# First four weight tiles turned by quarters beside the gradient's quarters; bias loads and row-table inverse later

## The chip, the cores and the metric

One core of a Trainium2 chip runs the whole program. The metric is device time in microseconds of one execution; lower is better. Three executions of the kernel before took 340.55 to 341.36 us, median 341.02.

A core has five engines that run side by side, each in the order of its own instruction list: TensorE (PE; its weight loads are shown as PEld), VectorE (DVE), ScalarE (ACT), GpSimd (POOL) and SyncE (SP), which issues most DMAs. An instruction that waits holds up everything behind it on its engine.

## The reference

The program computes a network block, forward and backward, for one sample x of S = 2048 rows and D = 448 columns, with a hidden width F = 1792. Cut to what matters:

```python
h  = x + irfft2(rfft2(layernorm(x)) * (w_r + 1j * w_i))        # spectral filter
u  = gelu(einsum("bsd,sf->bdf", layernorm(h), w1) + b1)        # mixes the rows (tokens)
y  = einsum("bdf,fs->bds", u, w2) + b2
out = h + transpose(y)
# outputs: out, and the gradients of x, w_r, w_i, w1, b1, w2, b2 for a given grad_out
```

The backward pass needs dgu = w2 applied to grad_out, that is, for every block j of 128 hidden units, the sum over all 16 row tiles t of w2[j, t] times grad_out[t]. This product needs nothing but inputs, so the kernel uses it as filler work for TensorE while the Fourier transforms are going.

## The kernel before

The Fourier transform along the 2048 rows is split in two, with tables of cosines and sines that the kernel computes itself (Sin on ScalarE). The program goes through these stages: the **row stage** (both first transforms, per tile t of rows, to about 49 us), the second transform and the filter (`s2_stage`), the inverse rows (`inv_rows`), the layer norm of h, the two products with w1 and w2, and then the backward pass through the same steps.

For TensorE, SyncE, VectorE and ScalarE the order of the instructions is the order in which the Python code writes them (`manual_schedule`, L155); a planner places GpSimd's only. What happens around the change:

- `xn` holds x, `go_tp` holds grad_out by row tiles; both are loaded in quarters of 4 tiles by SP at the start (`load_x` L325, `load_go` L328). x's first quarter comes as two halves (L331, L333).
- `w2Ts[j]` is block j of w2 with its rows and columns exchanged tile by tile ("turned"), 16 tiles of 128x128. `load_w2T` (L303) loads blocks 0 to 4 as they are (`N_NAT`, into rB), and TensorE turns them with `turn_w2` (L314): eight transposes into a PSUM buffer, then one ScalarE copy to rE or rO. From block 5 on, a transposing DMA loads them turned. A ring of five places holds the blocks, so block j + 5 is loaded once block j has been used. From the ninth on (`CAP`) these loads are held back until the row stage is over (L960 to L962).
- `dg_gen` (L828) issues the fillers: one 128x128 by 128x448 matmul for each (j, t). In it, `turns` (L830) says after which filler a block is turned, `order` (L831) goes over blocks 0 and 1 by quarters of t, and the rest block by block. `fill(n)` (L792) issues the next n fillers. `evac` (L184) moves a finished sum out of PSUM with ScalarE or VectorE, whichever has the smaller planned load.
- The row stage (L871 to L952) has for each row tile t: statistics (`ln_stats`, VectorE), a table scaled by the row's norm (`scale_R`, VectorE), a fold (`fold_prep` or `fold_quarters`, VectorE), `row_a` (L660: four matmuls, one evac), and three steps later `row_b` (L670: four matmuls, one evac, one reshuffling DMA by SP). `FILL_A` and `FILL_B` (L908, L909) say how many fillers go between.
- The tables of the column transform, `csF`, are made in two parts: `gen_fwd_d` (L438) computes angles on VectorE, and `cs_ops`, run at t = 1 (L933 to L936), puts a Sin on ScalarE, two mirrored copies on VectorE, and last a copy of one column on ScalarE (L454).
- `gen_RT` (L523) makes the inverse of the row table: four ScalarE copies (L904 to L907), one matmul, one evac; it runs at t = 2 (L949).
- `load_biases` (L813) loads b1 and b2 as rows; they are turned into columns later (`turn_biases`, L1026).
- 20 matmuls on zeros (L374) keep TensorE busy until the first data is there.
- PSUM has two sets of four buffers: `ps_ff` and `ps_mm`. A new tile waits until the tile that had its buffer is emptied.

Of the kernel before, what the change touches and what calls it, by code (L numbers as in the profile page):

```python
# [10 lines left out]
BF16 = mybir.dt.bfloat16  # L11
# [6 lines left out]
P = 128  # L18
S = 2048
D = 448  # L20
# [15 lines left out]
ML_F = 4  # L36
SIDE = 2
CAP = 9
N_NAT = 5
U_Q = 2  # L40
N_FILL_F = (6, 3, 20, 3, 24, 2)
N_FILL_B = (16, 16, 26, 8, 24, 8)
# [82 lines left out]
def kernel(  # L125
# [47 lines left out]
    def ring(reg, off, count, *dims):  # L173
        n = int(np.prod(dims))
        return Ring([cut(reg, off + i * n, *dims) for i in range(count)])
# [122 lines left out]

    x_pt = A_x[0].rearrange("(p t) d -> p t d", t=NT)
    go_pt_d = grad_out[0].rearrange("(p t) d -> p t d", t=NT)  # L300
    w2T_ring = Ring(ring(rE, 0, 3, NT, P).views + ring(rO, S, 2, NT, P).views)

    def load_w2T():  # L303
        j = w2T_ring.i
        if j == NFB:
            return
        wT = w2T_ring.next()
        w2Ts[j] = wT
        if j < N_NAT:
            nc.sync.dma_start(out=w2n[j], in_=B_w2[j * P:(j + 1) * P, :].rearrange("f (t c) -> f t c", c=P))  # L310
            return
        nc.sync.dma_start_transpose(out=wT, in_=B_w2[j * P:(j + 1) * P, :].rearrange("f (t c) -> f t c", c=P))

    def turn_w2(j, parts=((0, 8), (8, 8))):  # L314
        for h, n in parts:
            pt = (ps_mm if j < 2 else ps_ff)()[:].bitcast(BF16).rearrange("p (t c) -> p t c", c=P)
            for t in range(n):
                nc.tensor.transpose(pt[:, t, :], w2n[j][:, h + t, :], ident[:])
            sc.copy(out=w2Ts[j][:, h:h + n, :], in_=pt[:, 0:n, :])

    go_tp_d = grad_out[0].rearrange("(t p) d -> p t d", p=P)
    w2Ts = {}
    w2n = [cut(rB, j % 4 * S, NT, P) for j in range(N_NAT)]

    def load_x(q):  # L325
        nc.sync.dma_start(out=xn[:, 4 * q:4 * q + 4, :], in_=x_pt[:, 4 * q:4 * q + 4, :])
# [2 lines left out]
        nc.sync.dma_start(out=go_tp[:, 4 * q:4 * q + 4, :], in_=go_tp_d[:, 4 * q:4 * q + 4, :])  # L329

    nc.sync.dma_start(out=xn[:, 0:2, :], in_=x_pt[:, 0:2, :])  # L331
    load_w2T()
    nc.sync.dma_start(out=xn[:, 2:4, :], in_=x_pt[:, 2:4, :])  # L333
    load_go(0)
    load_w2T()
    load_x(1)
    load_go(1)
    load_go(2)
    load_go(3)
    load_w2T()  # L340
    load_x(2)
    load_w2T()
    load_x(3)
    gtail = rst[0:16, 2 * P:3 * P]
    gp_.memset(gtail, 0.0)
    nc.sync.dma_start(out=gtail[:, 0:64], in_=grad_out[0][S - 16:S, 3 * P:D])


    s1, s128, s2048 = 2.0 * _sin_scale(2), _sin_scale(128), _sin_scale(2048)
# [21 lines left out]
    sc.activation(out=warm, in_=warm, func=ACT.Sin)  # L371
    nc.vector.memset(rAT[:, 0:512], 0.0)
    idle = ps_mm()
    for _ in range(20):  # L374
        nc.tensor.matmul(idle[:, 0:D], lhsT=rAT[:, 0:P], rhs=rAT[:, 0:D], start=True, stop=True)

    pcol = col()
# [434 lines left out]

    def load_biases():  # L813
        gp_.memset(smr, 0.0)
        nc.sync.dma_start(out=smr[0:NFB, 0, :], in_=B_b1.rearrange("(j p) -> j p", p=P))
        nc.sync.dma_start(out=smr[:, 1, :], in_=B_b2.rearrange("(j p) -> j p", p=P))

        def turn():
            for i, dst in ((0, b1col), (1, b2col)):
                nc.sync.dma_start_transpose(out=smc[:, i, :], in_=smr[:, i, :])  # L820

        def place():
            for i, dst in ((0, b1col), (1, b2col)):
                ve.tensor_copy(out=dst[:], in_=smc[:, i, :])
        return turn, place


    def dg_gen():  # L828
        pgs = {}
        turns = {(0, 3): 1, (1, 11): 2, (2, 4): 3, (3, 4): 4}  # L830
        order = [(j, 4 * q + i) for q in range(4) for j in range(2) for i in range(4)]  # L831
        for j, t in order + [(j, t) for j in range(2, NFB) for t in range(NT)]:
            if not t:
                pgs[j] = ps_mm()
            mm(pgs[j][:, 0:D], lhsT=w2Ts[j][:, t, :], rhs=go_tp[:, t, :], start=(t == 0), stop=(t == NT - 1))
            if (j, t) in turns:
                turn_w2(turns[j, t], ((0, 4), (4, 4), (8, 8)) if j == 0 and t == 3 else ((0, 8), (8, 8)))
            if t == NT - 1:
                evac(out=dgu[:, j, :], in_=pgs.pop(j)[:, 0:D])
                if w2T_ring.i >= cap[0]:  # L840
                    held_w2.append(load_w2T)
                else:
                    load_w2T()
            yield
# [29 lines left out]
    fold_prep(xn, 0)  # L874
    ve.reciprocal(out=rstd_x[:, 0:2], in_=rstd_x[:, 0:2])
    Rs = {t: scale_R(t) for t in range(2)}
    turn_w2(0, ((0, 4), (4, 4)))
    row_a(0, Rs.pop(0))
    for t in range(2, 4):
        ln_stats(xn, t, mvx)  # L880
    sc.activation(out=rstd_x[:, 2:4], in_=mvx[:, 2:4, 1], func=ACT.Sqrt, bias=eps_x, scale=1.0)
    turn_w2(0, ((8, 8),))
    fold_prep(xn, 1)
    cs_ops = []
    gen_fwd_d(cs_ops)
# [3 lines left out]
    uv = gen_UV()  # L889
    gen_inv_cols(0)  # L890
    gen_inv_cols(1)
    fill(4)
    for t in (4, 5):
        ln_stats(xn, t, mvx)
    for fn in rstd_of(4, 6):
        fn()
    fill(0)
    turn_biases, place_biases = load_biases()
    Meter.side, Meter.every, Meter.count = [], 1, 0
    GROUPS = {0: (6, 8), 1: (8, 10), 3: (10, 12), 5: (12, 14), 7: (14, 16)}  # L900
    STATS = {0: (6, 7), 1: (8, 9), **{t: (t + 8,) for t in range(2, 8)}}
    INV_S = {10: 0, 11: 1, 12: 2, 13: 3}
    W_AT = {0: 2, 1: 1, 2: 2, 3: 1, 4: 2, **{t: 1 for t in range(5, 11)}, 11: 4}
    for c in range(2):  # L904
        for e in range(2):
            sc.copy(out=Rp.rearrange("p (e a q b c) -> p c e a q b", e=2, c=2, q=8, a=2)[:, c, e],
                    in_=Rm[:, 64 * c + 32 * e:64 * c + 32 * e + 32].rearrange("p (q a b) -> p a q b", q=8, a=2))  # L907
    FILL_A = (4, 4, 8, 12, 6, 3, 3, 3, 3, 3, 3, 3, 3, 3, 3, 3)  # L908
    FILL_B = (0, 0, 2, 2, 2, 2, 4, 4, 3, 2, 2, 2, 2, 2, 2, 2)  # L909
    for t in range(NT):  # L910
        if t == 0:
            load_w2T()
        if t + 1 < NT:
            row_a(t + 1, Rs.pop(t + 1))
        fill(FILL_A[t])
        if 1 <= t and t + 3 < NT:
            if t + 3 in (4, 8, 12):
                while Meter.side:
                    Meter.side.pop(0)()
            Rs[t + 3] = scale_R(t + 3)  # L920
        row_b(t - 3, csQ if t - 3 >= 4 * U_Q else None)
        if t == NT - 1:
            for i in range(t - 2, NT):
                row_b(i, csQ)
        if t % 2 and t < 12:
            if t // 2 + 2 < 2 * U_Q:
                fold_prep(xn, t // 2 + 2)
            else:
                fold_quarters(xn, t // 2 + 2, t // 2 % 2 * 2)
        if t == 4:  # L930
            for w in range(2):
                gp_.tensor_copy(out=csQ[:, w, :, :], in_=csF[:, w, 0, :].rearrange("p (j e) -> p e j", e=2))
        if t == 1:  # L933
            sc.activation(out=warm, in_=half_r, func=ACT.Sin, scale=1.0 / 64.0)
            while cs_ops:
                cs_ops.pop(0)()  # L936
        for i in STATS.get(t, ()):
            ln_stats(xn, i, mvx)
        for _ in range(3 if t > 0 else 0):
            if next(uv, None):  # L940
                break
        if t in GROUPS:
            a, b = GROUPS[t]
            newton_gp(mvx[:, a:b, 1], rstd_x[:, a:b], slice(a, b))
        for _ in range(W_AT.get(t, 0)):
            next(w_loads, None)
        if t in INV_S:
            gen_inv_s(INV_S[t])
        if t == 2:  # L949
            gen_RT()  # L950
        fill(FILL_B[t])
    for _ in uv:  # L952
# [7 lines left out]
    cap[0] = NFB  # L960
    while held_w2:
        held_w2.pop(0)()  # L962
    fill(14)

    def fwd_mult(s, j, x, y):
# [486 lines left out]
```

## Time and profile before

| | |
|---|---|
| median of 3 executions | 341.02 us (340.55 to 341.36) |
| the profiled execution: its time | 340.96 us |
| its span (first to last instruction) | 339.2 us |
| TensorE busy | 330.3 us (97%) |
| VectorE, ScalarE, GpSimd busy | 252.6, 206.2, 83.9 us |
| granted TensorE clock | 0.999 of full speed |
| moved by DMA | 78.03 MB |
| TensorE busy in 0:10, 10:20, 20:30, 30:40, 40:50 us | 8.09, 9.06, 9.80, 9.07, 10.00 us |

The page gives the busy time of each engine, a chain of work followed back from the last instruction, and groups of instructions; the trace behind it answers for any stretch of time what each engine did, what it waited for, and which instruction or transfer ended the wait. All times are microseconds from the start of the span. A matmul's length includes its way through the array, so successive matmuls overlap; what counts for the order of things is the distance from one start to the next.

### The profile page before, as it was taken

To read this page: it belongs to the slowest core of one execution; us is meant where nothing else is said; L and a number is where in the kernel's file an instruction comes from. 1 tells how busy PE (TensorE), PEld (TensorE's weight loads), DVE (VectorE), ACT (ScalarE), POOL (GpSimd) and SP (SyncE) were. 2 spreads that over 40 slices of the span, in tenths; PEclk is the share of its full clock that TensorE was granted. 3 is DMA by queue.
4 is the path that set the end of the run, shared out by engine and by line. 5 is a ranking of instruction groups with operands and counts; after the bars stand their busy time and mean duration, and the time that the engine had idled before them with its cause. 6 is when DMAs were issued, how large, how long until landed. Compare 5 with 4: busy or idle time off the path is not lost.

```text
span 339.2 us, 7995 instructions
## 1 busy us (share of the span) xinstructions
PE 330.3 (97%) x2893; PEld 174.0 (51%) x2893; DVE 252.6 (74%) x678; ACT 206.2 (61%) x447; POOL 83.9 (25%) x255
## 2 busy tenths in 40 slices
PE   8898999999999999999999999999999999999995
PEld 4565665456545555555555555555334344555552
DVE  8999649726947888594226988787598984599994
ACT  6886766858965544523132346665488875688882
POOL 7755602331310000000001111210002222156660
PEclk9999999999999999999999999999999999999999
DMA  7979999949999999787986989636998999969785
GB/s 250 399 195 183 228 245 196 167 110 261 252 366 305 337 277 241 179 259 197 187 192 154 188 176 165 171 83 203 262 254 280 184 227 281 349 164 295 233 309 198
DMA packets 136142, 78.03 MB, mean 230 GB/s; under 512 B 86568, under 2 KB 127512, under 8 KB 135976
## 3 DMA queue, kind: packets, MB, share of 16 engines
q1 hardware_dynamic: 133576, 73.59, 82.6%
q0 software_dynamic: 2528, 3.95, 5.5%
q8 instruction: 22, 0.36, 0.5%
q14 instruction: 16, 0.13, 0.2%
HBM read 28.33 MB, written 22.04 MB: 149 GB/s over the span
## 4 chain that ended last, share of the span: by engine, by line
PE 85%; DVE 6%; ACT 3%; DMA 2%; SPq 2%; issue 1%; POOL 0%; DVEq 0%; ACTq 0%
PE ps_mm L220 73%; PE ps_ff L220 8%; PE ps_ff L225 4%; DMA rA<-in_A_x_dram 2%; ACT rO L84 2%; DVE r L84 2%; DVE stats L84 1%; SPq L329 1%; SPq L310 1%; DVE rS L84 1%; DVE rA L84 1%; ACT rAT L84 0%; DVE rD L84 0%; DVE rX L84 0%; DVE rB L84 0%
## 5 line engine op out<-in xcount | busy, mean ns | idle before, releaser
L220 PEld LDWEIGHTS <-r 128*128 128x128 bf16 (+2 forms) x628 | 58.4, 104 | 47.6 <-issue 3.0
L220 PEld LDWEIGHTS <-rS 128*128 128x128 bf16 (+1 forms) x468 | 36.3, 97 | 33.4 <-issue 7.7
L84 ACT CAST rO<-ps_mm 128x512 bf16<-128x512 f32 (+1 forms) x69 | 36.9, 584 | 14.6 <-PE ps_mm L220 13.0
L220 PE MATMUL ps_mm<-rD,r 128*128 128x448 bf16 x224 | 44.5, 352 | 0.0
L220 PEld LDWEIGHTS <-rst 128*128 128x128 bf16 (+1 forms) x320 | 23.6, 97 | 31.3 <-issue 14.0
L731 POOL DMA_DIRECT2D r<-r x30 | 17.8, 601 | 66.5 <-ACT r L84 59.3
L220 PE MATMUL ps_mm<-rC,rE 128*128 128x448 bf16 x144 | 32.1, 353 | 0.5 <-DMA rC<-in_grad_out_dram 0.4
L220 PE MATMUL ps_mm<-rB,r 128*128 128x448 bf16 x160 | 31.2, 352 | 0.1
L220 PE MATMUL ps_mm<-rG,rst 128*128 128x512 bf16 (+1 forms) x128 | 28.7, 380 | 0.2 <-ACT rO L84 0.2
L220 PE MATMUL ps_mm<-r,rst 128*128 128x512 bf16 (+2 forms) x144 | 27.4, 345 | 0.0
L84 ACT ACTIVATE r<-ps_mm,rstd_h 128x448 bf16<-128x448 f32 x16 | 10.1, 633 | 26.8 <-PE ps_mm L220 26.8
L84 ACT CAST r<-ps_ff 128x452 bf16<-128x452 f32 x43 | 23.2, 589 | 4.5 <-PE ps_ff L225 2.1
L84 DVE SCALAR_TENSOR_TENSOR r<-ps_mm,b2col,r 128x448 bf16<-128x448 f32 x16 | 10.9, 682 | 19.9 <-PE ps_mm L220 19.8
L84 ACT ACTIVATE r<-rC 128x448 bf16<-128x448 bf16 x16 | 9.1, 571 | 26.7 <-DMA out_dram<-r 14.1
L1189 POOL TENSOR_SCALAR lcol<-lcol 128x1 f32<-128x1 f32 x16 | 8.5, 528 | 64.7 <-ACT r L84 64.7
L84 ACT ACTIVATE rG<-rG 128x896 bf16<-128x896 bf16 x14 | 13.3, 950 | 14.9 <-DVE rG L84 14.7
L220 PEld LDWEIGHTS <-rO 128*128 128x128 bf16 (+1 forms) x165 | 15.3, 98 | 12.2 <-ACT rO L84 0.2
L84 ACT CAST rS<-ps_ff 128x512 bf16<-128x512 f32 x31 | 18.1, 587 | 2.5 <-PE ps_ff L220 2.4
L220 PE MATMUL ps_ff<-csI,rAT 113*128 113x224 bf16 (+1 forms) x108 | 19.0, 298 | 0.4 <-ACT rAT L84 0.2
L84 DVE TENSOR_SCALAR rG<-rG 128x896 bf16<-128x896 bf16 x28 | 10.9, 388 | 10.0 <-ACT rG L84 10.0
L220 PE MATMUL ps_mm<-rC,rO 128*128 128x448 bf16 x80 | 18.1, 353 | 0.0
L84 ACT CAST rG<-ps_mm 128x512 bf16<-128x512 f32 (+1 forms) x28 | 13.8, 534 | 6.8 <-PE ps_mm L220 6.7
(202 smaller groups left out, 638.2 us busy)
## 6 DMA issues: line engine op xcount, KB each, us to landing
out_dram<-rO SPq DMA_DIRECT2D x34, 256.0 KB, 3.0
r<-in_B_w_dram SPq DMA_DIRECT2D x5, 1024.0 KB, 8.4
r<-r POOLq DMA_DIRECT2D x30, 113.0 KB, 5.4
out_dram<-rG SPq DMA_DIRECT2D x11, 256.0 KB, 3.7
r<-r SPq DMA_DIRECT2D x12, 226.0 KB, 2.5
r<-in_B_w_dram SPq DMA_DIRECT2D x3, 896.0 KB, 5.1
rS<-in_B_w_dram SPq DMA_DIRECT2D x3, 896.0 KB
rB<-in_B_w_dram SPq DMA_DIRECT2D x5, 512.0 KB, 9.8
```

The lines of the kernel that those rows point to most:

```text
L84: fn(**kw)
L220: nc.tensor.matmul(out, lhsT=lhsT, rhs=rhs, start=start, stop=stop)
L225: nc.tensor.matmul(out, lhsT=lhsT, rhs=rhs, start=start, stop=stop)
L310: nc.sync.dma_start(out=w2n[j], in_=B_w2[j * P:(j + 1) * P, :].rearrange("f (t c) -> f t c", c=P))
L329: nc.sync.dma_start(out=go_tp[:, 4 * q:4 * q + 4, :], in_=go_tp_d[:, 4 * q:4 * q + 4, :])
L731: defer(RESH_LAG, lambda g=g, ab=ab, eng=eng: eng.dma_start(out=D3[rowbase(g):rowbase(g) + 29:4, :, :, :], in_=ab), ab)
L1189: gp_.tensor_scalar(out=m1, in0=ms, scalar1=-1.0 / D, scalar2=None, op0=ALU.mult)
```

## The change

Blocks 0 to 3 of w2 are now loaded in eight pieces, each a quarter of the columns (4 tiles) of a pair of blocks, and these loads stand between the quarters of x and grad_out. Each piece is turned by eight transposes into one PSUM buffer (now always `ps_ff`) and one ScalarE copy with two 512-wide blocks (the first piece has two copies). The fillers go over all four blocks quarter by quarter, so four sums stay open at once, and a piece or two are turned after fillers 7, 15, 31 and 47 (counted from 0). Block 4 is still loaded whole and is turned in two halves, after fillers 57 and 61. The order of places in the ring changes accordingly. Of the 20 matmuls on zeros 10 stay, and 2 new ones stand behind the first piece's transposes. The first 4 fillers now come ahead of `row_a(0)`. The copies for the inverse row table and `gen_RT` go to step t = 13. The loads of the biases and of the last 16 rows of grad_out (`gtail`) are issued after the row stage, behind the loads of w2 that were held back. `FILL_A` and `FILL_B` are new.

```diff
-N_NAT = 5
+N_QTR = 4
...
-    w2T_ring = Ring(ring(rE, 0, 3, NT, P).views + ring(rO, S, 2, NT, P).views)
+    w2T_ring = Ring(ring(rE, 0, 2, NT, P).views + ring(rO, S, 2, NT, P).views + [cut(rE, 2 * S, NT, P)])
...
+    def turned():
+        return ps_ff()[:].bitcast(BF16).rearrange("p (t c) -> p t c", c=P)
+
+    def turn_half(h):
+        pt = turned()
+        for t in range(8):
+            nc.tensor.transpose(pt[:, t, :], w2n4[:, h + t, :], ident[:])
+        sc.copy(out=w2Ts[N_QTR][:, h:h + 8, :], in_=pt)
+
+    def turn_quarter(k):
+        q, p = divmod(k, 2)
+        pt = turned()
+        for t in range(8):
+            nc.tensor.transpose(pt[:, t, :], w2q[:, 2 * p + t // 4, 4 * q + t % 4, :], ident[:])
+        dst = w2pair[p][:, :, 4 * q:4 * q + 4, :]
+        if k:
+            sc.copy(out=dst, in_=pt.rearrange("p (j t) c -> p j t c", j=2))
+            return
+        for j in range(2):
+            sc.copy(out=dst[:, j], in_=pt[:, 4 * j:4 * j + 4, :])
+
+    def load_quarter(k):
+        q, p = divmod(k, 2)
+        src = B_w2[2 * p * P:(2 * p + 2) * P, :].rearrange("(j f) (t c) -> f j t c", f=P, c=P)
+        nc.sync.dma_start(out=w2q[:, 2 * p:2 * p + 2, 4 * q:4 * q + 4, :], in_=src[:, :, 4 * q:4 * q + 4, :])
...
     nc.sync.dma_start(out=xn[:, 0:2, :], in_=x_pt[:, 0:2, :])
-    load_w2T()
+    load_quarter(0)
+    load_go(0)
     nc.sync.dma_start(out=xn[:, 2:4, :], in_=x_pt[:, 2:4, :])
-    load_go(0)
-    load_w2T()
+    load_quarter(1)
     load_x(1)
     load_go(1)
+    load_quarter(2)
+    load_quarter(3)
+    load_x(2)
     load_go(2)
+    load_quarter(4)
+    load_quarter(5)
+    load_x(3)
     load_go(3)
-    load_w2T()
-    load_x(2)
-    load_w2T()
-    load_x(3)
+    load_quarter(6)
+    load_quarter(7)
...
-    nc.sync.dma_start(out=gtail[:, 0:64], in_=grad_out[0][S - 16:S, 3 * P:D])
...
-    for _ in range(20):
+    for _ in range(10):
         nc.tensor.matmul(idle[:, 0:D], lhsT=rAT[:, 0:P], rhs=rAT[:, 0:D], start=True, stop=True)
...
-        turns = {(0, 3): 1, (1, 11): 2, (2, 4): 3, (3, 4): 4}
-        order = [(j, 4 * q + i) for q in range(4) for j in range(2) for i in range(4)]
+        turns = {7: (1,), 15: (2, 3), 31: (4, 5), 47: (6, 7)}
+        order = [(j, 4 * q + i) for q in range(4) for j in range(N_QTR) for i in range(4)]
...
+            for k in turns.get(n, ()):
+                turn_quarter(k)
+            if n in (57, 61):
+                turn_half(2 * (n - 57))
...
-    turn_w2(0, ((0, 4), (4, 4)))
+    turn_quarter(0)
+    for _ in range(2):
+        nc.tensor.matmul(idle[:, 0:D], lhsT=rAT[:, 0:P], rhs=rAT[:, 0:D], start=True, stop=True)
+    fill(4)
     row_a(0, Rs.pop(0))
...
-    turn_w2(0, ((8, 8),))
...
-    fill(4)
...
-    turn_biases, place_biases = load_biases()
...
-    FILL_A = (4, 4, 8, 12, 6, 3, 3, 3, 3, 3, 3, 3, 3, 3, 3, 3)
-    FILL_B = (0, 0, 2, 2, 2, 2, 4, 4, 3, 2, 2, 2, 2, 2, 2, 2)
+    FILL_A = (4, 7, 9, 7, 1, 6, 2, 5, 4, 3, 3, 3, 3, 3, 3, 3)
+    FILL_B = (0, 0, 0, 0, 5, 3, 6, 4, 3, 2, 2, 2, 2, 2, 2, 2)
...
-        if t == 2:
+        if t == 13:
+            for c in range(2):
+                for e in range(2):
+                    sc.copy(out=Rp.rearrange("p (e a q b c) -> p c e a q b", e=2, c=2, q=8, a=2)[:, c, e],
+                            in_=Rm[:, 64 * c + 32 * e:64 * c + 32 * e + 32].rearrange("p (q a b) -> p a q b", q=8, a=2))
             gen_RT()
...
     while held_w2:
         held_w2.pop(0)()
+    turn_biases, place_biases = load_biases()
     fill(14)
```

## The prediction, on record before the run

> **What bounds the kernel now.** I read the share of busy time by engine first, then the chain that ended last, then who made TensorE wait, then the timelines of the first 35 us engine by engine.
>
> ```profile
> span 339.2 us, 7995 instructions
> PE 330.3 (97%) x2893; PEld 174.0 (51%) x2893; DVE 252.6 (74%) x678; ACT 206.2 (61%) x447; POOL 83.9 (25%) x255
> ...
> PE 85%; DVE 6%; ACT 3%; DMA 2%; SPq 2%; issue 1%; POOL 0%; DVEq 0%; ACTq 0%
> ```
>
> TensorE is busy 330.3 of 339.2 us: a time is lost or won only where PE idles. The waits of PE alone (line, releaser, total, times, longest):
>
> ```profile
> PE ps_ff L220 <- DVE rS L84: 1.8, 2, 1.0
> PE ps_mm L375 <- DVE rS L627: 1.2, 1, 1.2
> PE ps_mm L220 <- DMA rC<-in_grad_out_dram: 0.4, 1, 0.4
> ```
>
> Almost all of it lies before 31 us, in the row stage that the change rewrites. There the chain is no longer PE's: between 16.4 and 32.8 us nearly every link is VectorE's. Now the timelines (start, length, engine, line, what; in brackets the idle time before it). PE:
>
> ```profile
> 12.69 1.68 PE L220 MATMUL ps_mm<-rC,rE 128*128 128x448 bf16 x8
> ...
> 15.57 0.65 PE L220 MATMUL ps_ff<-rX,rS 128*128 128x128 bf16 x4 [0.78 <-DVE rS L84]
> ...
> 17.46 2.05 PE L220 MATMUL ps_mm<-rC,rE 128*128 128x448 bf16 x10
> ...
> 30.81 0.38 PE L220 MATMUL ps_ff<-rX,rS 128*128 128x128 bf16 x4 [1.01 <-DVE rS L84]
> ```
>
> ScalarE and VectorE:
>
> ```profile
> 14.64 0.57 ACT L84 ACTIVATE csF<-r 128x452 bf16<-128x452 f32 x1
> 16.29 0.20 ACT L84 COPY csF<-rAT 128x2 bf16<-128x2 bf16 x1 [1.08 <-DVE csF L84]
> 16.39 0.58 ACT L84 CAST rS<-ps_ff 128x512 bf16<-128x512 f32 x1
> ...
> 17.50 1.95 ACT L84 COPY rE<-ps_ff 128x1024 bf16<-128x1024 bf16 x2
> ```
> ```profile
> 6.19 1.15 DVE L84 BATCH_NORM_STATS2 stats<-rA 128x6 f32<-128x448 bf16 x2 [0.20 <-DMA rA<-in_A_x_dram]
> ...
> 10.28 0.42 DVE L84 TENSOR_SCALAR rX<-Rm,rstd_x 128x128 bf16<-128x128 bf16 x2
> ...
> 15.74 0.46 DVE L84 TENSOR_SCALAR csF<-csF,cols 128x224 bf16<-128x224 bf16 x2
> ```
>
> The reader is to see one thing: ScalarE works in order, and at 16.29 its tiny csF copy (cs_ops, L454) has waited 1.08 us for VectorE's mirrored table (15.74 to 16.20). Everything queued behind it on ScalarE starts after 16.39. VectorE has no slack before that: it is busy 8.5 of the first 10 us and 9.3 of the next. In the old kernel this holds nobody up, because PE has whole turned tiles 0 and 1 to multiply (the x8 at 12.69).
>
> **The change, part by part.** I count fillers (matmuls of dg_gen, issued 0.189 us apart: ten of them from 17.46 to 19.35) as n. A row_a takes 0.22 us of PE, a row_b 0.39, eight transposes 0.45 (sixteen from 20.54 to 21.43).
>
> *Dummies, 20 to 12; order of loads.* The dummies end at 6.6 us; ten would end near 4.6, and the first filler could start near 6.3 instead of 8.19. This earns nothing: the changed order on PE is 4 fillers, row_a 0 and 1, 4 fillers, quarter 1, row_a 2, which PE reaches at about 8.8; row_a 2 needs the scaled table that VectorE makes at 10.28. PE waits there.
>
> *x rows 2 and 3.* They now stand behind the first gradient quarter: 224+256+448+224 = 1152 KB up to their end, 960 before. In the DMA issues of before they land at 1.66+4.5 = 6.16 (960 KB) and the gradient quarter at 2.13+5.9 = 8.03 (1408 KB). By KB between the two: 6.16 + 192/448 x 1.87 = 6.96, so d = 0.8 us later, an estimate; the ends are d = 0 and d = 1.9 (quarter rows of 1 KB have no row in this trace; the 896-byte gradient is the nearest, the range covers it). VectorE waits for these rows at 6.19 already, so d moves all of its chain. x rows 8 to 11 come earlier and save VectorE the 0.24 us it waited at 16.4, but after csF.
>
> *The turn by quarters.* Filler 16 needs quarter 2, turned after filler 15. PE gets there at 10.5+d: row_a 2, 7 fillers, row_a 3, 1 filler, 16 transposes (2.8 us) bring it to about 13.3+d. In the changed order on ScalarE the copy of quarter 2 stands behind the table load, csF, the csF copy and the copy of row_a 3. So: csF copy 16.29+d, next at 16.39+d, row_a 3's cast 0.48 (16.39 to 16.86 before), copy of quarter 2 0.97 (two in 1.95; bounds for its two-block output: 0.95, and 1.07 as two of 512), PE at 17.9+d = 18.7. **PE idles about 4.5 us.** Queued behind that matmul on PE: row_a 4, row_b 0, all later turns.
>
> What that costs I take by work, not by idle time. At 18.7 the old PE had issued 24 + (18.7-17.46)/0.189 = 30.6 fillers, 5 row_a, 48 transposes and the inverse; the new one 16, 4 and 32. Behind by 14.6 x 0.189 + 0.22 + 0.89 + 0.06 = 3.9 us.
>
> *Two smaller waits of the same kind.* Filler 32 needs quarter 4, turned right before: on ScalarE row_b 0's cast 0.44, Ut 0.64, row_a 5's cast 0.48 and the copy 0.97 lie after row_b 0, with 0.2 us of handing over 2.7 us; PE meanwhile has row_a, one filler, 16 transposes and row_b: 1.7. Wait 1.0. Filler 48: copy 0.97+0.2 against 0.84 of PE work: 0.4 with row_a 7's cast ahead. Bounds: 0 and 2 for both.
>
> *What goes.* The 1.01 us at 30.81 and 0.1 after it: row_a 9 used the buffer of a turned half whose copy stood behind Vt on ScalarE (29.50); now it takes row_a 8's, emptied by VectorE. VectorE's two dgu casts (1.06 us at 21.33) go to ScalarE, one row_b cast (0.54) comes back; VectorE is not what PE waits for then. Minus 1.1.
>
> *What is hidden.* The same 80 transposes and ten tile-halves' worth of copies. Bias and gradient-tail loads: three small issues leave SP at 10.5 to 13.2 and stand among the held weight loads near 50 us, ahead of three of them; SP idles from 60.5 to 71.7, and SP turns the biases only at 85.2. Row-table inverse: four ScalarE copies (0.60), one matmul, one cast (0.27) move from 11.7 to row step 13; first read at 76.1. The five transposed loads that ring slots gate now follow fillers 51 to 63, with two reshuffles behind them on SP (2.1 to 2.5 us each); filler 80 then comes some 3 us after its tile. Without that cover: up to 2 us.
>
> **Sum:** 3.9 + 1.0 + 0.4 - 1.1 = +4.2 us. After 49 us PE has almost no gap to absorb this. The profiled execution took 340.96 us (span 339.2 and 1.8 around it), which is 0.06 below the median 341.02: 340.96 + 4.2 = **345.2 us**.
>
> **Rivals.**
> *1. PE runs slow again after the gap.* Rows: the twenty dummies took 5.42 us; less the 0.35 of the last, 19 spacings of 0.267 against 0.189 later, 1.5 us lost at the start although the granted clock reads 1.00. The longest PE gap after that is 1.01 us, and matmuls behind it still come 0.19 apart. A gap of 4.5 is beyond what the trace shows. If the start is paid again: 4.2 + 1.5, 346.7 us. The Trainium skill, "TensorE: Matmul & The Clock Gate", part 1, "What's actually happening", says that TensorE falls to half rate after an idle window of about 3.4 us and that the window runs free; by that rule this gap may or may not hold a whole window. The same page shows a fall 5.2 us after the last matmul, in "Seeing it yourself"; no run here shows either yet.
> *2. ScalarE doesn't hold quarter 2* (csF's turn comes early enough). Then filler 16 starts near 14.9+d, and the next waits are VectorE's row tables for row_a 5 and quarter 4 behind them; carried through with the same durations, PE is about 2.6 us behind: 343.6. Against it: VectorE's order up to csF is unchanged.
> *3. Faster: VectorE's chain stays the bound.* From 16.4 to 32.8 it is the chain; it loses 1.06 + 0.24 and gains 0.54. If PE catches up before row_a 9, the end comes 0.76 - d earlier: at d = 0, 340.2. It decides if filler 16 starts before about 14.9, where the old PE waited too. The csF row speaks against it.
> *4. It does nothing:* the lag is used up in later waits. PE has 50.0 busy us of every 50 from 100 to 250. About 341.
>
> **How the numbers follow.** Chances: forecast 0.55, rival 1 0.24, rival 2 0.10, rival 3 0.06, rival 4 0.05. Range: d = 0 and the small waits at 0.4 lower give 344.0, rival 2 343.6, so low 343.0; d = 1.7 with rival 1 gives 347.6, so high 347.8. About 0.2% is what a measurement can tell from no change. Faster 0.06, same 0.05, slower 0.89.
>
> **What would show it.** Right: PE idle of 4 to 5 us ahead of a ps_mm<-rC,rE matmul near 14 us, released by ScalarE's rE copy; ScalarE idle over 2 us before its csF copy, released by VectorE; VectorE waiting near 1 us for rA at 6 us; row_a 9 near 35 instead of 30.81; the 32x32 matmuls starting near 53.4 instead of 49.2, and from there to the end the old length. Rival 1: fillers over 0.3 apart behind the gap. Wrong: fillers flowing by 15 us, or the new lag gone again after 60 us.

## The result, and the profile after

The changed kernel takes **351.19 us** (median of four executions, 348.67 to 354.26) against 340.85 in the comparison (340.55 to 341.36, four executions). The ratio is 1.027, 95% interval 1.022 to 1.032. Ratios here and below leave out executions more than 1.5% above the fastest of the same kernel (here the one at 354.26), so they are not quite the quotients of the medians. The forecast said slower, 345.2 us, in a range of 343.0 to 347.8: the direction holds, the size is outside the range. The profiled execution took 351.88 us, 10.9 more than the 340.96 of before.

The page after: span, busy time by engine, the granted clock in 40 slices, and the engines' shares of the chain that ended last.

```profile
span 350.1 us, 7983 instructions
...
PE 333.8 (95%) x2885; PEld 175.4 (50%) x2885; DVE 253.6 (72%) x679; ACT 206.8 (59%) x445; POOL 84.7 (24%) x255
...
PEclk9889999989999999999999999999999999999999
...
PE 86%; ACT 4%; DVE 4%; DMA 2%; issue 2%; SPq 1%; POOL 0%; ACTq 0%
```

PE is busy 3.5 us longer with eight matmuls fewer, and idles 7.4 us more (350.1 - 333.8 against 339.2 - 330.3). In the clock line an 8 stands at slices 1, 2 and 8 (counted from 0); before, every slice had a 9. So there are two losses, waits and slower matmuls. PE's waits after:

```profile
PE ps_mm L220 <- ACT rE L84: 3.8, 3, 2.6
PE ps_ff L220 <- DVE rX L84: 2.6, 1, 2.6
PE ps_ff L225 <- issue: 2.5, 2, 1.9
PE ps_mm L403 <- DVE rS L655: 1.2, 1, 1.2
PE ps_ff L220 <- ACT rO L84: 0.9, 1, 0.9
```

The 1.8 of the old first line (PE waiting for VectorE's rS) is gone, and four waits have come. Their places, in PE's timeline:

```profile
11.93 0.55 PE L220 MATMUL ps_ff<-rX,rS 128*128 128x128 bf16 x4 [2.60 <-DVE rX L84]
...
19.25 3.16 PE L220 MATMUL ps_mm<-rC,rE 128*128 128x448 bf16 x8 [2.62 <-ACT rE L84]
...
26.98 1.12 PE L220 MATMUL ps_mm<-rC,rE 128*128 128x448 bf16 x5 [0.94 <-ACT rE L84]
...
32.58 1.31 PE L220 MATMUL ps_mm<-rC,rE 128*128 128x448 bf16 x6 [0.27 <-ACT rE L84]
...
36.94 0.39 PE L220 MATMUL ps_ff<-rX,rS 128*128 128x128 bf16 x4
...
48.33 0.23 PE L220 MATMUL ps_ff<-ident,rO 128*128 128x128 bf16 x1 [0.89 <-ACT rO L84]
...
56.96 0.63 PE L225 MATMUL ps_ff<-r,Vt 32*32 32x452 bf16 x16 [0.64 <-issue]
...
75.97 0.31 PE L225 MATMUL ps_ff<-rS,UTn 32*32 32x226 bf16 x14 [1.89 <-issue]
76.22 3.68 PE L220 MATMUL ps_mm<-rC,rE 128*128 128x448 bf16 x11
```

In order: row_a 2 waits for its scaled table; filler 16, 32 and 48 wait for ScalarE's copies of quarters 2, 4 and 6; row_a 9 (36.94, before 30.81) no longer waits; the inverse row table's matmul waits for its four copies; the second transform starts at 56.96 (before 49.20). The x8 at 19.25 starts its matmuls 0.37 apart (it ends in a row_a at 22.20), and so does the x11 at 76.22 from its fifth on; at full clock they are 0.19 apart. ScalarE and VectorE around filler 16:

```profile
14.52 0.57 ACT L84 ACTIVATE csF<-r 128x452 bf16<-128x452 f32 x1
17.60 0.20 ACT L84 COPY csF<-rAT 128x2 bf16<-128x2 bf16 x1 [2.51 <-DVE csF L84]
17.70 0.58 ACT L84 CAST rS<-ps_ff 128x512 bf16<-128x512 f32 x1
18.18 1.02 ACT L84 COPY rE<-ps_ff 128x1024 bf16<-128x1024 bf16 x1
```
```profile
7.47 1.15 DVE L84 BATCH_NORM_STATS2 stats<-rA 128x6 f32<-128x448 bf16 x2 [1.52 <-DMA rA<-in_A_x_dram]
...
11.59 0.44 DVE L84 TENSOR_SCALAR rX<-Rm,rstd_x 128x128 bf16<-128x128 bf16 x2
...
17.05 0.46 DVE L84 TENSOR_SCALAR csF<-csF,cols 128x224 bf16<-128x224 bf16 x2
```

This is the chain of the forecast link by link: x rows 2 and 3 land late (7.47 against 6.19, so d = 1.3), VectorE's tables move by 1.3, ScalarE waits 2.51 us at the csF copy, then does row_a 3's cast, then quarter 2.

The windows view cut along the steps in which the granted clock changes here (3.41 us each; columns: length, PE busy, matmuls, clock, DMA share, GB/s):

```profile
8.62:12.03 3.41, 0.81 (x12) 1.00 1.06 381
12.03:15.44 3.41, 3.41 (x16) 0.50 1.08 382
15.44:18.86 3.42, 1.18 (x18) 1.00 1.08 378
18.86:22.27 3.41, 3.02 (x9) 0.50 1.16 251
...
73.47:76.88 3.41, 1.52 (x52) 1.00 0.77 130
76.88:80.30 3.42, 3.42 (x11) 0.50 0.35 94
```

Three windows are at half rate, and each follows one in which PE was busy for 0.81, 1.18 and 1.52 of 3.41 us.

**The account of the profiled execution.** Row_a 9 is 6.13 late: the half-rate window at 18.86 took 1.5 of it (half of 3.02 busy us), and the rest, 4.6, is put down to the waits. From there to the second transform 0.89 for the inverse table, 0.64 for the start of that transform, 0.1 in small pieces. At 74 stands a wait of 1.89 that the profile calls "issue", which means that nothing it shows ended it; the longest such wait of before is 0.35, at 66.43: 1.5. The window behind it costs 1.7. Sum 4.6 + 1.5 + 1.6 + 1.5 + 1.7 = 10.9. The window at 12.03 cost nothing of its own: slow matmuls filled time in which PE would have waited for quarter 2 anyway, which is why that wait is 2.62 and not 4.5 (with a full clock, in the fourth run below, filler 16 starts no earlier).

### The profile page after: what moved, and what is told of

It reads as the page before. It is cut to its first block, busy times and chain, and to the rows that moved or that the text cites. A ratio compares the mean times of both kernels' runs of the same rounds, so it can differ in the third digit from the quotient of the medians.

```text
span 350.1 us, 7983 instructions
## 1 busy us (share of the span) xinstructions
PE 333.8 (95%) x2885; PEld 175.4 (50%) x2885; DVE 253.6 (72%) x679; ACT 206.8 (59%) x445; POOL 84.7 (24%) x255
## 4 chain that ended last, share of the span: by engine, by line
PE 86%; ACT 4%; DVE 4%; DMA 2%; issue 2%; SPq 1%; POOL 0%; ACTq 0%
PE ps_mm L220 73%; PE ps_ff L220 8%; PE ps_ff L225 4%; ACT rO L84 2%; DMA rA<-in_A_x_dram 2%; DMA r<-r 1%; DVE stats L84 1%; ACT rE L84 1%; DVE rA L84 1%; DVE r L84 1%; ACT rAT L84 0%; DVE rS L84 0%; ACT r L84 0%; ACT rS L84 0%; PE ps_ff L322 0%
## 5 line engine op out<-in xcount | busy, mean ns | idle before, releaser
L84 ACT CAST r<-ps_ff 128x452 bf16<-128x452 f32 x41 | 22.1, 589 | 8.1 <-PE ps_ff L220 2.8
L220 PEld LDWEIGHTS <-rO 128*128 128x128 bf16 (+1 forms) x181 | 17.7, 101 | 16.3 <-issue 1.9
L84 DVE SCALAR_TENSOR_TENSOR r<-ps_mm,b2col,r 128x448 bf16<-128x448 f32 x16 | 10.9, 682 | 19.9 <-PE ps_mm L220 18.1
L220 PE MATMUL ps_mm<-rC,rO 128*128 128x448 bf16 x96 | 22.7, 373 | 0.0
L84 ACT CAST rS<-ps_ff 128x512 bf16<-128x512 f32 x29 | 16.8, 581 | 8.9 <-PE ps_ff L220 8.8
L220 PEld LDWEIGHTS <-rE 128*128 128x128 bf16 x128 | 11.7, 103 | 14.3 <-ACT rE L84 5.2
L84 DVE TENSOR_SCALAR rG<-rG 128x896 bf16<-128x896 bf16 x28 | 10.9, 389 | 10.0 <-ACT rG L84 10.0
```

The source lines that it names most:

```text
L84: fn(**kw)
L220: nc.tensor.matmul(out, lhsT=lhsT, rhs=rhs, start=start, stop=stop)
```

## Experiments: the waits and the clock in the new order

Theory after the result: the waits came as worked out (about 5 to 6 us with the inverse table), and the rest is the clock falling behind short gaps. Rivals: the waits are larger than worked out, from one of three moved things (the csF copy ahead of quarter 2, the late inverse table, the x rows behind the gradient); or something after 49 us costs on its own. The first three runs take away one of these each, the fourth keeps what causes the waits and fills the gaps with matmuls whose results nobody uses.

Each ratio is to executions of the kernel before from the same comparison: median 342.29 for the first four runs, 341.64 for the next four, 341.10 for the last four. They spread more than the four above, from 340.17 to 347.33 us, with mean clocks from 1.000 down to 0.990.

**The csF column copy later on ScalarE**, behind quarter 2 and 3:

```diff
+        if t == 2:
+            cs_ops.pop(0)()
...
-            while cs_ops:
+            while len(cs_ops) > 1:
                 cs_ops.pop(0)()
```

> The changed kernel, with only the last of cs_ops (the one-column copy of csF on ScalarE) moved from step 1 to step 2, behind the copies of quarters 2 and 3. Theory (ScalarE's order holds quarter 2 behind VectorE's mirrored table): the 2.62 us wait ahead of filler 16 shrinks below 1 us and the half-clock stretch that begins at 18.9 us goes; row_a 5 and filler 32 then wait somewhat longer. Time about 351.2 - 2.5 = 348.7 (347.5 to 350). Rival (VectorE's late tables are the bound, ScalarE's order only names the wait): the lost time moves to row_a 4 and 5, and the time stays within 0.7 us of 351.2.

Measured: 349.01 us, ratio 1.0185 (1.011 to 1.026). The wait for quarter 2 is gone (0.41 us left, at 17.20, for the gradient's rows), so that copy was what held filler 16. The time is near the 348.7 that was expected (347.5 to 350). But about half of the wait comes back one quarter later; PE's timeline of this kernel:

```profile
24.90 1.12 PE L220 MATMUL ps_mm<-rC,rE 128*128 128x448 bf16 x5 [1.99 <-ACT rE L84]
...
74.30 0.31 PE L225 MATMUL ps_ff<-rS,UTn 32*32 32x226 bf16 x14 [3.05 <-issue]
```

Filler 32 now waits 1.99 instead of 0.94. It still starts 2.1 earlier than in the changed kernel (24.90 against 26.98), and 1.5 of that is the half-rate window at 18.86, which is gone. The issue wait at 74 is 3.05 here, followed by a half-rate window, as is the wait for row_a 2 (2.47). Two half-rate windows in all.

**The inverse table's copies at step 10 instead of 13**, the matmul still at 13:

```diff
-        if t == 13:
+        if t == 10:
             for c in range(2):
...
+        if t == 13:
             gen_RT()
```

> The changed kernel, with the four ScalarE copies for the inverse row table at step 10 instead of 13 (its matmul stays at 13). Theory (this wait of 0.89 us at 48.3 us is on the path): it goes, and the time falls by 0.9 to about 350.3. Rival (the second transform's first matmuls wait for the reshuffled rows anyway, 0.64 us there): the wait moves there, and the time stays at 351.2 within 0.4.

Measured: 350.86 us, ratio 1.0239 (1.015 to 1.033). The 0.89 us wait is gone, and the wait at the start of the second transform stays (0.77). From row_a 9 to that start it takes 19.2 us (38.59 to 57.78) instead of 20.0 (36.94 to 56.96), so 0.8 of the 0.9 is gained there. In this execution filler 16 waited 4.30 us at 19.58 with a full clock before it, which is the 4.5 of the forecast seen bare; two half-rate windows come with it (18.47 to 25.30) and hide a gain of this size in the total: 350.86 lies between the 350.3 of the theory and the 351.2 of the rival.

**x rows 2 and 3 ahead of the first gradient quarter:**

```diff
-    load_go(0)
     nc.sync.dma_start(out=xn[:, 2:4, :], in_=x_pt[:, 2:4, :])
+    load_go(0)
```

> The changed kernel, with x rows 2 and 3 loaded ahead of the first gradient quarter (behind quarter 0 of the weights). Theory (d, the late landing of these rows, moves VectorE's whole chain): VectorE waits under 0.3 us for them instead of 1.52, row_a 2 starts near 10.7 instead of 11.9, its gap on PE shrinks below 1 us because the gradient lands later, so no half-clock stretch begins at 12 us; the csF copy comes near 16.4 and filler 16 near 18. Time about 351.2 - 1.3 - 0.5 = 349.4. Rival (the row stage's losses don't reach the end; what counts lies after 57 us): within 0.5 of 351.2.

Measured: 351.85 us, ratio 1.0259 (1.016 to 1.036): no gain, where 349.4 was expected. What the load order was to do did happen: row_a 2 starts at 10.53 instead of 11.93, and filler 16 at 17.86 instead of 19.25, both 1.4 earlier. It was taken back by the clock: the wait for quarter 2 is 3.99 us, two half-rate windows come with it (16.48 to 23.30), and one more follows an issue wait of 2.78 at 77. A gain of 1.4 us in waits cannot be read from a total that carries up to three such windows.

**Matmuls in the gaps**, 13 ahead of row_a 2 and 18 behind the transposes of quarters 2 and 3:

```diff
+        if t == 1:
+            for _ in range(13):
+                nc.tensor.matmul(idle[:, 0:D], lhsT=rAT[:, 0:P], rhs=rAT[:, 0:D], start=True, stop=True)
...
+            if n == 15:
+                pw = ps_ff()
+                for _ in range(18):
+                    nc.tensor.matmul(pw[:, 0:D], lhsT=rAT[:, 0:P], rhs=rAT[:, 0:D], start=True, stop=True)
```

> The changed kernel, with matmuls on zeros put into the two long gaps on PE: 13 ahead of row_a 2 and 18 behind quarter 3's transposes. Theory (a gap of over 1.9 us in a window of 3.41 us halves the clock for the next window): both half-clock stretches of the row stage go; the one at 12 us was hidden in the next wait, the one at 19 us cost 1.5 us; time about 349.6. Rival (the slow stretches are hidden behind VectorE and ScalarE): 351.2 within 0.5. Were the clock no matter and the added matmuls late, slower by up to 1 us.

Measured: 346.99 us, ratio 1.0140 (1.006 to 1.022), and the clock stays full until the last stage: the mean is 0.999 or 1.000 in all four executions. With 31 matmuls more, the median is 4.2 us below that of the changed kernel; the two intervals (1.006 to 1.022, 1.022 to 1.032) meet only at their ends. The theory expected 349.6: it had counted the window at 18.86 alone, and this profiled execution has neither the issue wait near 74 nor the window behind it. PE's timeline, and VectorE's first wait:

```profile
19.59 1.69 PE L220 MATMUL ps_mm<-rC,rE 128*128 128x448 bf16 x8 [0.89 <-ACT rE L84]
...
35.80 0.39 PE L220 MATMUL ps_ff<-rX,rS 128*128 128x128 bf16 x4
...
47.19 0.23 PE L220 MATMUL ps_ff<-ident,rO 128*128 128x128 bf16 x1 [0.89 <-ACT rO L84]
...
55.12 0.48 PE L225 MATMUL ps_ff<-r,Vt 32*32 32x452 bf16 x16
```
```profile
7.84 1.15 DVE L84 BATCH_NORM_STATS2 stats<-rA 128x6 f32<-128x448 bf16 x2 [1.90 <-DMA rA<-in_A_x_dram]
```

Filler 16 starts no earlier (19.59), since it waits for ScalarE, yet row_a 9 is at 35.80: 5.0 late. The second transform is 5.92 late (55.12 - 49.20), and the end too (span 345.1 against 339.2). So **the waits alone cost 5.9 us**, all of it before 56 us, and in this execution nothing after 56 us costs on its own. Of the 5.9, the inverse table is 0.9; the other 5.0 are the forecast's 4.2 with the d of this execution, 7.84 - 6.19 = 1.65 instead of 0.8.

**The three changes together**, without and with matmuls in the gaps (4 behind quarter 3, 9 behind quarter 5):

```diff
-    load_go(0)
...
+    load_go(0)
...
+        if t == 2:
+            cs_ops.pop(0)()
...
-            while cs_ops:
+            while len(cs_ops) > 1:
...
-        if t == 13:
+        if t == 10:
...
+        if t == 13:
             gen_RT()
```
```diff
+            if n in (15, 31):
+                pw = ps_ff()
+                for _ in range(4 if n == 15 else 9):
+                    nc.tensor.matmul(pw[:, 0:D], lhsT=rAT[:, 0:P], rhs=rAT[:, 0:D], start=True, stop=True)
```

> The changed kernel with three edits at once: csF's column copy behind quarters 2 and 3, the inverse table's ScalarE copies at step 10, x rows 2 and 3 ahead of the first gradient quarter. Theory (what was lost is the sum of these waits, and each half-clock window of 3.41 us adds about 1.5 us): no gap over 1 us before filler 32, one gap of about 2 us there; the row stage ends near 51.7 us. 343.0 with full clock, 344.5 with one half-clock window; median 343 to 345. Rival (quarter by quarter over four tiles costs in itself, by its transposes and loads): 347 or more.

> As the kernel with three edits, and matmuls on zeros behind quarter 3's (4) and quarter 5's transposes (9), so that the gap ahead of filler 32 is filled. Theory (the clock falls only when a window is mostly idle): full clock from the start on, the fillers 0.19 us apart throughout, 343.0 to 343.5, and a smaller spread than without. Rival (the gap at filler 32 is too short to matter for the clock): the same time as without the dummies, or up to 0.5 more.

Measured: 349.06 us, ratio 1.0143 (1.007 to 1.021), and 346.75 us, ratio 1.0135 (1.009 to 1.018). Both miss what was expected (343 to 345, and 343.0 to 343.5); the first lies where its rival put it. In the first the gradient's first quarter is now late (a wait of 3.24 at 8.92), two half-rate windows come with it and a third at 55.64, behind a wait of 2.67 at the start of the second transform; its four executions run from 345.17 at a mean clock of 1.000 to 351.36. In the second the profiled execution (344.89 us, the fastest of the four) has a full clock and, after 1.52 us for the gradient at 8.26, waits of 0.8 us or less in the row stage; the other three, 346.42 to 349.03, have mean clocks of 0.993 to 0.999. PE reaches the second transform at 51.9, as expected (51.7), but waits there:

```profile
53.66 0.63 PE L225 MATMUL ps_ff<-r,Vt 32*32 32x452 bf16 x16 [1.75 <-issue]
```

The profile names no releaser, but the rows can be followed: SyncE issues the third of the four reshuffles of the last row tiles at 47.62, it lands at 53.57, and PE starts 0.09 later. The same 0.09 lies between the third reshuffle and PE in the four other executions of the new order with a wait here: the changed kernel (landed 56.87), and the runs with the copies at step 10 (57.69), with the x rows first (56.98) and with the three changes without matmuls in the gaps (56.01). In the two without a wait it had landed 0.15 us or more ahead. So this wait is for the reshuffled rows. That the profiled execution is 1.9 us above the 343.0 of the theory is nearly all this wait; that the new order costs something in itself besides (the rival) is not ruled out for the other executions.

## Experiments: the old order

**Only the late inverse table and the late bias and gradient-tail loads**, on the kernel before:

```diff
-    nc.sync.dma_start(out=gtail[:, 0:64], in_=grad_out[0][S - 16:S, 3 * P:D])
...
-    turn_biases, place_biases = load_biases()
...
-        if t == 2:
+        if t == 13:
+            for c in range(2):
+                for e in range(2):
+                    sc.copy(out=Rp.rearrange("p (e a q b c) -> p c e a q b", e=2, c=2, q=8, a=2)[:, c, e],
+                            in_=Rm[:, 64 * c + 32 * e:64 * c + 32 * e + 32].rearrange("p (q a b) -> p a q b", q=8, a=2))
             gen_RT()
...
+    turn_biases, place_biases = load_biases()
```

> The kernel before, with one part of the change alone: the inverse row table (its ScalarE copies and matmul) at step 13, and the loads of the biases and the gradient's tail behind the held weight loads. Theory (the matmul waits for copies that stand right ahead of it on ScalarE): PE waits 0.9 us for rO near 42 us, and the time rises by 0.9 to about 341.8. Rival (the part is hidden, as predicted): within 0.3 of before.

Measured: 342.53 us, ratio 1.0004 (0.997 to 1.003). The wait for the four copies is there (1.02 us at 42.01), and the second transform starts at 49.93, 0.7 later than before. The interval, about 1 us to either side, holds both the 0.9 of the theory and the rival's 0.3, so the total decides nothing.

**Only the old stall at row_a 9 removed**, by turning block 4 six fillers earlier:

```diff
-        turns = {(0, 3): 1, (1, 11): 2, (2, 4): 3, (3, 4): 4}
+        turns = {(0, 3): 1, (1, 11): 2, (2, 4): 3, (2, 14): 4}
```

> The kernel before, with block 4 turned after filler 46 instead of 52, so that its two ScalarE copies stand ahead of the Vt activation that waits for VectorE. Theory (the 1.01 us ahead of row_a 9 comes from copies held behind Vt): that wait goes, row_a 9 comes near 29.8, and the time falls by 0.7 to 1.0, to 340.0. Rival (VectorE's chain is right behind, or the copies then delay row_a 7's cast): the wait moves to row_a 8 or 9 and the time stays within 0.3 of before.

Measured: 342.92 us, ratio 1.0022 (0.999 to 1.006): no gain. The 1.01 us wait is gone, and PE reaches the second transform earlier, but:

```profile
51.08 0.62 PE L225 MATMUL ps_ff<-r,Vt 32*32 32x452 bf16 x16 [2.86 <-DMA r<-rX]
```

It waits 2.86 us for rows that SyncE's reshuffling DMAs have yet to land, and starts 1.9 later than before (49.20). SyncE issued the four from 43.58 on, 0.9 later than before (42.72), and the reshuffles from 36 us on take 5.3 to 6.3 us to land, where before took 3.9 to 4.7 (the trace shows three of six landings in each).

**The same with one transposed load of w2 fewer ahead of the reshuffles** (the block is loaded after the row stage instead):

```diff
-CAP = 9
+CAP = 8
...
-        turns = {(0, 3): 1, (1, 11): 2, (2, 4): 3, (3, 4): 4}
+        turns = {(0, 3): 1, (1, 11): 2, (2, 4): 3, (2, 14): 4}
```

> The old order with block 4 turned earlier (as in e8), and one transposed load of w2 (4 MB of descriptors' time, 2 to 2.5 us on SyncE's queue near 36) held back until the row stage is over, behind the reshuffles of the last rows. Theory (the second transform starts when the reshuffled rows have landed, about 1 us after the burst of loads, so what stands ahead of them on SyncE sets it): the reshuffles issue 2 us earlier, the 32x32 matmuls start at 48 to 49 instead of 51.08, and the wait of 2.86 us goes: 340.0 to 341.0, ratio 0.995 to 0.999 to the kernel before. The block held back is needed about 15 us later, so it may give back up to 1 us there. Rival (the start is set by the row stage's own last products): 49.2 or later and no gain over e8, ratio 1.002.

(The "4 MB" in it is a slip: a block of w2 is 128 x 2048 bf16, 0.5 MB.) Measured: 340.94 us against 341.10, ratio 0.9996 (0.997 to 1.003). SyncE issues the first of the four reshuffles at 39.77 instead of 43.58 (the first line is of the run above, the second of this one):

```profile
43.58 3.35 SPq L693 DMA_DIRECT2D r<-rX  x4
39.77 6.10 SPq L693 DMA_DIRECT2D r<-rX  x4
```

PE's timeline has

```profile
48.91 0.41 PE L225 MATMUL ps_ff<-r,Vt 32*32 32x452 bf16 x16
...
51.05 2.44 PE L220 MATMUL ps_mm<-rC,rO 128*128 128x448 bf16 x12 [0.51 <-DMA rO<-in_B_w_dram]
```

The second transform starts 2.2 us earlier than in the run above and 0.3 earlier than before, and the wait for the rows is gone. Their place on SyncE is the smaller part of it: the third reshuffle, the one that PE waited for, is issued only 0.4 earlier (44.69 against 45.08). The larger part is that, with one load of w2 fewer ahead of them, the reshuffles land 2.2 to 4.2 us after their issue (again three of six) instead of 5.3 to 6.3. The 0.3 is given back at once by a wait of 0.51 for the block that was held. So in the old order the tables, the reshuffled rows and the next block of w2 stand close behind one another, and removing one wait showed the next; the totals of all three runs agree with before within their intervals. No version tried here beats the kernel before.

## Experiments: a gap by itself

The three kernels below are the one before with one gap put into a stretch, near 150 us, where PE is otherwise never idle: a small matmul waits for memsets on GpSimd that nothing else needs.

```diff
+    gap = mem.tile([P, P], BF16, name="gap")
+    gp_.memset(gap[:], 0.0)
...
+            if t == 6:
+                pw = ps_ff()
+                nc.tensor.matmul(pw[:, 0:P], lhsT=gap[:], rhs=gap[:], start=True, stop=True)
+                for _ in range(9):
+                    gp_.memset(gap[:], 0.0)
+                nc.tensor.matmul(pw[:, 0:P], lhsT=gap[:], rhs=gap[:], start=True, stop=True)
```

The second has, behind the memsets' lines, 14 matmuls `nc.tensor.matmul(pw[:, 0:D], lhsT=w2cs[3][:, 0, 0:P], rhs=g_[:, 0, :], start=True, stop=True)`; the third has 20 memsets and no such matmuls.

> The kernel before, with one gap put into TensorE's fully busy stretch near 150 us: a matmul that waits for nine small GpSimd memsets (estimated 2.6 us from memsets of 0.28 each and 0.2 of handing over); nothing else waits for them. Nothing of the computation is left out. Theory (a granted-clock window of 3.41 us that was idle by 1.9 us or more is followed by one at half rate): +2.6 us for the gap, and 1.7 more in about two executions of three, those where the gap does not fall across the border of two windows; so the median near 341.0 + 4.3 = 345.3, single executions at 343.6 or 345.3, and a segment at 0.5 in the trace if the profiled one is of the second kind. Rival (only a wholly idle window slows the clock, or the clock cost nothing in the changed kernel): +2.6 in all executions, 343.6, clock full.

> The same wait, with fourteen matmuls of 128x448 (0.19 us each, results unused) in front of the matmul that waits, so that TensorE is busy through it. Theory and rival both: about 14 x 0.19 = +2.7 us, 343.7, clock full, single executions within 0.5 of each other. Theory: 1.6 below the median of the gap left empty. Rival: no difference from it.

> The same wait with twenty memsets, an estimated 5.3 us. Theory: at least one window is idle by 2.6 us whatever the phase, and two in a part of the executions: +5.3 + 1.7 = 348.0, up to 349.7 in some. Rival of the wholly idle window: 5.3 us hold a whole window of 3.41 in about half of the executions, so 346.3 or 348.0. Rival of no clock cost: 346.3 always.

Measured: 345.49 us for the single gap (343.24 to 349.52, ten executions; ratio 1.0101, 1.006 to 1.014), 347.14 for the filled one (344.77 to 354.53, four; ratio 1.0137, 1.006 to 1.021), 349.65 for the double (348.49 to 350.41, four; ratio 1.0222, 1.016 to 1.029).

The medians of the first two do not tell theory and rival apart, the filled gap is not the faster one as the theory had it, and its executions lie 9.8 us apart instead of 0.5. The mean clocks of the single gap's executions fit the theory's 1.7: three with 0.995 took 345.62 to 346.57, five with 0.997 or more 343.24 to 345.35, though among those two at 1.000 took 344.44 and 345.24, more than the 343.6 expected. The traces say why the medians do not settle it. In the single gap's profiled execution (343.24 us) the gap of 2.42 fell across the border of two windows:

```profile
151.60:155.00 3.40, 2.24 (x13) 1.00 0.81 240
155.00:158.42 3.42, 2.17 (x13) 1.00 0.58 169
```

Both were over 2.1 us busy, no window was slowed, and the execution is 2.3 us longer than the one of before (340.96): the gap alone. In the filled gap's (349.10 us) PE did not idle at the edit at all, but at 69 us, where its code is that of before:

```profile
69.30 0.28 PE L225 MATMUL ps_ff<-rS,UVT 32*32 32x226 bf16 x5 [3.23 <-issue]
```

That is 2.9 more than the 0.35 of before, plus 1.7 for the half-rate window that follows, plus 2.8 for the added matmuls: 7.4 of the 8.1 more. The double gap separates the theories in its trace:

```profile
155.48:158.89 3.41, 1.03 (x7) 1.00 0.65 198
158.89:162.30 3.41, 0.49 (x3) 0.50 0.35 101
162.30:165.72 3.42, 3.42 (x11) 0.50 0.00 0
```

A gap of 5.30 us gave two slow windows, although no window was wholly idle (1.03 and 0.49 us busy). The profiled cost, 350.41 - 340.96 = 9.45, is 5.3 for the gap, 1.95 for the 3.9 busy us at half rate behind it, 1.9 for an issue wait at 68.43 (2.23 against 0.35), and 0.3 that no row explains.

## Why the prediction was right and where it failed

- *Dummies, start of fillers: right.* PE waits 2.60 for row_a 2's table; the working gives 2.3 to 2.5 (10.28 or 10.5, plus 0.8, less 8.8). So the earlier start earned nothing.
- *x rows: right in kind, short in size.* d was 1.3 here and 1.65 in the run with filled gaps, for an estimated 0.8. It lay within the stated ends of 0 and 1.9.
- *The turn by quarters: right.* ScalarE's 2.51 us before the csF copy, then the cast, then quarter 2, as written; taking the copy out of the way removes the wait. The idle 4.5 us were 4.30 and 3.99 in two runs with a full clock ahead of them, 2.62 here.
- *The small waits: right*, 0.94 and 0.27 for 1.0 and 0.4. *The old stall goes: right* in the new order; undone alone in the old order it earns nothing that can be told (0.9996 to 1.0022).
- *The sum up to row_a 9: right.* 4.2 with d = 0.8 is 5.05 with d = 1.65, and 4.99 were measured at full clock.
- *What is hidden: failed at two items.* The inverse row table was priced at 0 because it is read only at 76.1. But its matmul stands in PE's order at step 13 behind four ScalarE copies issued just ahead of it, and PE waits 0.89. When a result is needed is not what counts for an engine that works in order. And the transposed loads with reshuffles behind them were weighed only by when filler 80 would find its tile. The reshuffles themselves landed late: 0.64 at the start of the second transform here, nothing in the run with filled gaps, 1.75 in the one with all three changes and filled gaps.
- *Rival 1: the step that put the time outside the range.* The sum has no term for the clock. The rival that had one was held to be less likely than not (0.24), to happen once, behind the 4.5 us gap, for 1.5 us. The clock fell three times in the profiled execution, for 3.2 us besides the part hidden in a wait, and first behind the gap ahead of row_a 2, which the rival had not looked at. The assumption beneath was "The longest PE gap after that is 1.01 us, and matmuls behind it still come 0.19 apart": true, but the limit lies near 1.8 us of idle time within a window, not near 4.5. The sign set for the rival, fillers over 0.3 apart behind the gap, is the one seen (0.37). Without the clock's part the kernel is inside the range (346.99 with filled gaps); its fastest execution, with one half-rate window's worth of lost clock, is outside it (348.67).
- *"From there to the end the old length": wrong for the profiled execution* by 3.2 us, the issue wait at 74 and the half-rate window behind it. The runs give no sign that this is the change's doing: such a wait stands in the profiled execution of three of the seven kernels in the new order and of three of the seven in the old. The kernels with a gap put in near 150 us differ from the one before, ahead of that, only by one memset of 0.19 us on GpSimd at 2.69; in their profiled executions they had no such wait, 3.23 and 2.23. It comes in some executions and not in others.

Of the 10.9 us of the profiled execution the sum had 4.2. The 6.7 that it lacked are 3.2 for the clock, 1.5 for the issue wait, 0.9 for the inverse table, 0.6 for the late rows, 0.4 for d and 0.1 in small pieces.

The parts check against the other executions by an estimate: a half-rate window lowers the mean clock of 350 us by 0.5 x 3.41 / 350 = 0.005 and costs up to 1.7 us. The fastest execution (348.67, mean clock 0.994) is then 340.9 + 5.9 + one window; the one at 350.51 (0.990) has two. What the slowest (354.26, 0.985) spent beyond three windows stays open, as only one execution has a trace.

## What to carry to other kernels

Price a gap on a nearly always busy TensorE by the window it falls in, not by its length alone: once about half of 3.4 us is idle, each such window costs up to 1.7 us more. Unused matmuls in front of the waiting one avoided that in the row stage (31 of them, 4.2 us); for the single gap near 150 us no gain could be told. Before moving a small step later "because it is read late", look at what stands next to it in each engine's own order, and put its parts some steps apart. Where several waits stand close behind one another, removing one may earn nothing; look for the next one (here the reshuffled rows, which land later behind the loads of w2) before starting.

## What the runs showed of the hardware

**The clock.** Over the fourteen traces, the granted clock changes only on a grid of 3.41 us whose phase differs from execution to execution. Every window at full rate with PE busy for 1.52 us or less (twelve between the start and the last stage, 0.23 to 1.52) was followed by one at half rate; every one with 1.62 or more was not. Busy is as this view counts it, transposes and small matmuls included. One of the two cases at 1.62, from the old order with block 4 turned earlier:

```profile
46.60:50.01 3.41, 1.62 (x9) 1.00 1.04 340
50.01:53.42 3.41, 2.34 (x56) 1.00 1.21 160
```

So by this count the limit lies between 1.52 and 1.62 us of 3.41. A half-rate window that was busy for 2.93 us or more brought the full rate back; one busy for 0.49 to 2.35 us was followed by a second (four cases). The Trainium skill, "TensorE: Matmul & The Clock Gate", part 1, "What's actually happening", has the free-running window of about 3.4 us and the half rate, and the traces agree (3.41 us, 0.50). It gives one idle window as the condition; here a window with 1.9 of 3.41 us idle was enough, and the measurement decides. Because the phase is free, the same gap can cost nothing or up to 1.7 us more, and that spreads the times: 348.67 to 354.26 for the changed kernel. It is not the only thing that does: the kernel before, with no gap over 1.3 us in its trace, took 340.55 to 341.36 in four executions and 340.17 to 347.33 in all, some at a mean clock of 0.990 to 0.995. Those have no trace; a wait like the one below, and a half-rate window behind it, would fit.

**Waits that the profile calls "issue".** PE waited 1.4 to 3.2 us near 68 to 77 us, among the small 32x32 matmuls, in the profiled execution of six of fourteen kernels, old order and new. That code is the same in all of them, and in four of the six a half-rate window followed. What ends these waits is not shown, and no run here tested it.
